# A two-stage kernel (gated linear attention, then an MLP): attention in chunks of 64 tokens of two batch rows, its products in quarter and half tiles of the array, TensorE in written order

## Chip, core, metric

One core of a Trainium2 chip runs the whole program. Its engines work side by side and wait for each other by semaphores: TensorE (PE, matrix products into PSUM; a product is a load of a stationary operand of up to 128 rows and 128 columns, PEld in the profile, and a pass of moving columns over it), VectorE (DVE), ScalarE (ACT), GpSimd (POOL) and SyncE (SP, which here only issues DMAs). The metric is device time in microseconds, lower is better.

## What is computed

For 4 batch rows and 8 heads an mLSTM cell with a 40x40 state runs over 768 tokens; its output, gated, goes through a two-layer MLP with SiLU. Cut to what matters:

```python
for t in range(S):
    m_new = np.maximum(f_gate[:, :, t] + m, i_gate[:, :, t])
    f_stab = np.exp(f_gate[:, :, t] + m - m_new)
    i_stab = np.exp(i_gate[:, :, t] - m_new)
    m = m_new
    C = f_stab[..., None, None] * C + i_stab[..., None, None] * np.einsum('bhd,bhe->bhde', vt, kt)
    n = f_stab[..., None] * n + i_stab[..., None] * kt
    h = np.einsum('bhde,bhe->bhd', C, qt)
    denom = np.maximum(np.abs(np.einsum('bhd,bhd->bh', n, qt)), 1.0)[..., None]
    y[:, :, t] = h / (1.0 + np.exp(-o_gate[:, :, t])) / denom
x = y.transpose(0, 2, 1, 3).reshape(3072, 320)
h = x @ w_in                                   # 320 x 2048
out = (h / (1.0 + np.exp(-h))) @ w_out         # 2048 x 320
```

All data are f32; the answer is f32.

## The kernel before

The recurrence is done by chunks. A *unit* is 128 tokens of one batch row with all 8 heads; there are 24 (6 chunks by 4 batch rows; unit n is chunk n // 4 of batch row n % 4). Per unit and head, *scores* multiply k by q (L392; 128 tokens of k by 128 of q), VectorE multiplies them with the tile D of decays (L411), and *values* multiply the weighed D with v that carries a column of ones (41 columns, L431). From the second chunk on the product of decayed q with the carried state Cm is added in the same PSUM tile (L422). *State* multiplies k with the decayed v (L461; three heads to a product, of which only the diagonal blocks are wanted, so VectorE masks them with bm, L487), and Cm is decayed and summed up on GpSimd (L472, L488). D starts as a broadcast DMA of the log decays (L277); GpSimd masks it (L353) and ScalarE takes eight exponentials with a bias each (L363). The 8 first units (LIGHT) keep q and k in f32 in 40 of 64 rows, half the heads in each half of the rows; all later units split q and k into a rounded part and a remainder (ScalarE L336, VectorE L338), stacked to 120 rows, so that one product of the fp32r kind does.

VectorE turns a unit's values into x: nq, den, the division, the output gate and a copy (L437 to L453). Three *transposes* (L494) and a split into two fp32r parts (L496, L497) hand x to the MLP.

The MLP works in 8 *steps* of 3 units (384 tokens). A step has 16 chunks fc of 128 hidden columns. The first products of a chunk are 8 (L526, 384 moving columns, called mm1), the second ones, two chunks later, 9 (L566, 320 moving columns, called mm2; in step 0 three in plain f32). Between them ScalarE and VectorE make th, gh and gl (L530 to L546; in step 0 only th and g).

Weights come as float64 bits and are unpacked by VectorE and ScalarE in 18 parts (L182 to L217; wti and wto are its tiles); the calls are written in front of the loop over steps and within the first chunks of step 0.

What sets the order: SyncE's DMAs go in written order. The other engines are put in order by the framework's scheduler, which works with priorities and its own estimates of duration. The units are cut in 5 pieces (`piece`, L611), and a table SCHED says how many pieces are due by which chunk of which step. Tiles come from rotating pools; psA, which holds scores, values, state and transposes, has three PSUM banks.

## Time and profile before

| | us |
|---|---|
| device time, median of 3 runs (526.55 to 527.87) | 527.78 |
| span of the profiled execution, first to last instruction | 521.3 |
| TensorE busy (matmul / weight load) | 482.5 / 462.5 |
| VectorE, ScalarE, GpSimd busy | 343.1, 267.8, 98.6 |
| first MLP product | 60.4 |
| first second product of step 1 | 134.3 |
| last matmul ends | 516.96 |

The page gives no time for the profiled execution but its span; what the runs show above it (6.5 us to the median) lies before the first and after the last instruction. The ends of matmuls are modelled and overlap the next one's start, so the cost of a group is read from the start of its first to the start of the next group. An f32 product stands in the trace as two pairs of load and matmul, an fp32r product as one.

### The profile page before, as it was taken

To read this page: it belongs to the slowest core of one execution; us is meant where nothing else is said; L and a number is where in the kernel's file an instruction comes from. 1 tells how busy PE (TensorE), PEld (TensorE's weight loads), DVE (VectorE), ACT (ScalarE), POOL (GpSimd) and SP (SyncE) were. 2 spreads that over 40 slices of the span, in tenths; PEclk is the share of its full clock that TensorE was granted. 3 is DMA by queue.
4 is the path that set the end of the run, shared out by engine and by line. 5 is a ranking of instruction groups with operands and counts; after the bars stand their busy time and mean duration, and the time that the engine had idled before them with its cause. 6 is when DMAs were issued, how large, how long until landed. Compare 5 with 4: busy or idle time off the path is not lost.

```text
span 521.3 us, 8616 instructions
## 1 busy us (share of the span) xinstructions
PE 482.5 (93%) x3086; PEld 462.5 (89%) x3086; DVE 343.1 (66%) x717; ACT 267.8 (51%) x647; POOL 98.6 (19%) x139
## 2 busy tenths in 40 slices
PE   1477899999999979998999999999999999999996
PEld 1376878788989969998999999999999999999996
DVE  6579999945777678586865866449575745454332
ACT  1554776532765556575465564446464433334332
POOL 0121232231333422332203211121210000000000
PEclk9999999999999999999999999999999999999999
DMA  4999975163476385746513543433570100001001
GB/s 108 319 322 265 273 268 157 40 183 93 124 188 183 108 201 150 214 127 155 157 67 106 156 105 107 115 108 104 152 209 18 28 14 26 0 2 39 0 2 38
DMA packets 52525, 65.54 MB, mean 126 GB/s; under 512 B 3195, under 2 KB 40479, under 8 KB 52483
## 3 DMA queue, kind: packets, MB, share of 16 engines
q1 hardware_dynamic: 48963, 60.95, 41.6%
q10 hardware_dynamic: 3520, 4.04, 2.2%
q8 instruction: 24, 0.39, 0.3%
q14 instruction: 18, 0.15, 0.1%
HBM read 60.94 MB, written 4.04 MB: 125 GB/s over the span
## 4 chain that ended last, share of the span: by engine, by line
PE 59%; DMA 19%; DVE 11%; ACT 5%; issue 2%; SPq 1%; POOL 1%; POOLq 0%; ACTq 0%; DVEq 0%
PE ph L526 25%; PE pout L566 24%; DMA D<-LFd 12%; PE po L431 5%; DMA raw<-in_qk_dram 4%; DVE st L338 3%; ACT D L363 3%; PE ps L392 2%; DMA kvo<-in_kvo_dram 2%; PE po L422 2%; POOL D L353 1%; DVE D L411 1%; ACT st L336 1%; PE px L494 1%; PE pu L461 1%
## 5 line engine op out<-in xcount | busy, mean ns | idle before, releaser
L526 PE MATMUL ph<-xh,wh 128*128 128x384 f32 x384 | 136.1, 354 | 3.3 <-DVE th L539 2.3
L526 PE MATMUL ph<-xl,wh 128*128 128x384 f32 x384 | 130.6, 340 | 0.0
L566 PE MATMUL pout<-woh,gh 128*128 128x320 f32 x336 | 106.6, 319 | 3.0 <-ACT gh L544 3.0
L539 DVE SCALAR_TENSOR_TENSOR th<-th,ph 128x384 f32<-128x384 f32 x112 | 61.5, 549 | 70.1 <-ACT th L530 69.8
L566 PE MATMUL pout<-wol,gh 128*128 128x320 f32 x336 | 103.2, 309 | 0.0
L566 PE MATMUL pout<-woh,gl 128*128 128x320 f32 x336 | 100.4, 313 | 1.3 <-DVE gl L545 1.2
L545 DVE TENSOR_TENSOR gl<-th,gh 128x384 fp32r<-128x384 f32 x112 | 65.0, 582 | 54.3 <-ACT gh L544 52.4
L530 ACT ACTIVATE th<-ph 128x384 f32<-128x384 f32 x128 | 62.0, 485 | 62.2 <-PE ph L526 61.0
L526 PE MATMUL ph<-xh,wl 128*128 128x384 f32 x256 | 87.4, 342 | 0.0
L544 ACT CAST gh<-th 128x384 fp32r<-128x384 f32 x112 | 57.1, 510 | 51.2 <-DVE th L539 49.6
L526 PEld LDWEIGHTS ph<-xh,wh 128*128 128x128 f32 x384 | 73.0, 190 | 6.7 <-DVE th L539 3.4
L526 PEld LDWEIGHTS ph<-xl,wh 128*128 128x128 f32 x384 | 73.0, 190 | 0.6
L363 ACT ACTIVATE D<-D,aT 128x128 f32<-128x128 f32 x192 | 59.8, 390 | 17.1 <-POOL D L353 17.0
L566 PEld LDWEIGHTS pout<-woh,gh 128*128 128x128 f32 x336 | 63.2, 188 | 4.9 <-ACT gh L544 4.8
L566 PEld LDWEIGHTS pout<-woh,gl 128*128 128x128 f32 x336 | 61.7, 188 | 2.6 <-DVE gl L545 2.3
L566 PEld LDWEIGHTS pout<-wol,gh 128*128 128x128 f32 x336 | 63.2, 188 | 0.1
L431 PEld LDWEIGHTS po<-kvo,D 128*128 128x128 f32 x384 | 53.3, 215 | 3.3 <-ACT wh L203 2.1
L431 PE MATMUL po<-kvo,D 128*128 128x41 f32 x384 | 54.3, 299 | 1.9 <-ACT wh L203 1.9
L353 POOL TENSOR_SCALAR_AFFINE_SELECT D<-D 128x512 f32<-128x512 f32 x48 | 36.8, 790 | 91.6 <-ACT fd L350 66.2
L338 DVE TENSOR_TENSOR st<-raw,st 40x512 fp32r<-40x512 f32 x64 | 45.9, 717 | 7.1 <-ACT st L336 5.6
L526 PEld LDWEIGHTS ph<-xh,wl 128*128 128x128 f32 x256 | 48.7, 190 | 0.0
L336 ACT CAST st<-raw 120x512 fp32r<-120x512 f32 x64 | 35.7, 621 | 17.0 <-DMA raw<-in_qk_dram 17.0
(74 smaller groups left out, 548.2 us busy)
## 6 DMA issues: line engine op xcount, KB each, us to landing
raw<-in_qk_dram SPq DMA_DIRECT2D x32, 480.0 KB
D<-LFd SPq DMA_DIRECT2D x24, 512.0 KB
kvo<-in_kvo_dram SPq DMA_DIRECT2D x24, 484.0 KB
wro<-in_w_out_dram SPq DMA_DIRECT2D x8, 640.0 KB
wri<-in_w_in_dram SPq DMA_DIRECT2D x8, 512.0 KB
out_dram<-ob ACTq DMA_DIRECT2D x24, 160.0 KB
qt<-in_qp_dram SPq DMA_DIRECT2D x20, 180.0 KB
lq<-LFd SPq DMA_DIRECT2D x60, 60.0 KB
```

Source lines behind the costliest of these rows:

```text
L336: nc.scalar.copy(t, raw)
L338: nc.vector.tensor_tensor(out=t[r0 : r0 + D, :], in0=raw[r0 : r0 + D, :], in1=t[r0 : r0 + D, :].bitcast(F32), op=ALU.subtract,)
L353: nc.gpsimd.affine_select(out=d, in_=d, compare_op=ALU.is_ge, fill=NEG, base=0, pattern=[[0, HH], [1, L]], channel_multiplier=-1,)
L363: nc.scalar.activation(d[:, h, :], d[:, h, :], AF.Exp, bias=aT[:, c, r + h : r + h + 1])
L392: nc.tensor.matmul(ps[:, j, :], k_[:, cs], q_[:, cs], start=True, stop=True)
L431: nc.tensor.matmul(po[:, h, :], self.Dm[:, h, :], self.vt[:, h, :], start=first, stop=(h == H - 1))
L526: nc.tensor.matmul(ph, w, x, start=(i == 0), stop=(i == len(ops) - 1))
L530: nc.scalar.activation(th, ph, AF.Tanh, scale=0.5)
L539: nc.vector.scalar_tensor_tensor(out=th, in0=th, scalar=1.0, in1=ph, op0=ALU.add, op1=ALU.mult)
L544: nc.scalar.copy(gh, th)
L545: nc.vector.tensor_tensor(out=gl, in0=th, in1=gh.bitcast(F32), op=ALU.subtract)
L566: nc.tensor.matmul(self.po[t], g[:, ts], w, start=(fc == 0 and i == 0), stop=(last and i == len(ops) - 1),)
```

## The change

A unit is now 64 tokens of two batch rows (a pair p), again 128 rows, with 8 heads of each; there are again 24 (12 chunks by 2 pairs; unit n is chunk n // 2 of pair n % 2), so the carried state passes from unit n to unit n + 2 in place of n + 4. The 16 (batch row, head) combinations are laid out in 8 slots; everything stays f32 and the split of q and k is gone.

- *Scores* (L376 of the changed kernel): 16 products of 64x64 tokens; heads lie in two halves of the rows and batch rows in two halves of the columns. D is 128x8x64, half as large.
- *Values* (L408): 8 products whose stationary operand has 64 columns, written to one half of the PSUM rows; the moving operand v holds the two batch rows block-wise, the other block zero, 2x41 columns. The carried state is a product of the same form (qt against Cm, 104 rows).
- *State* (L443): 8 products with 40 stationary columns; here k, not v, is decayed (kw). No mask is needed. Decaying Cm stays on GpSimd (L456), the addition moves to VectorE (L462).
- *Decay*: `shift` adds mask and gates on GpSimd ahead of time, `decay` adds the loaded log decays, one exponential does all 8 heads.
- q comes once; the decayed q is made from the same tile, so the load of qp is gone. k with o, and v, are loaded apart; outputs are stored by two DMAs.
- *Order*: from the loop over steps on TensorE runs in the order in which the program is written. `piece` k = 0 of unit n now issues the scores of unit n + 1 and then values and state of unit n; k = 1 the transposes; `shift` and `decay` are for unit n + 2. The scores of unit 3 move ahead of the loop.

On TensorE, one unit within a later step; pu, po, ps, px, ph and pout are state, values, scores, transposes, mm1 and mm2. Before (values of one unit, a group of mm1 and its state; its transposes and the scores of the next unit stand elsewhere):

```order
L422 MATMUL po_2269<-Cm_106,qt_1773 128x123 x2
L422 MATMUL po_2269<-Cm_106,qt_1773 128x82
L431 MATMUL po_2269<-kvo_1771,D_1765 128x41 x8
L566 MATMUL pout_2_2151<-wol_1229,gh_3_2173 128x320
L566 MATMUL pout_2_2151<-woh,gl_3_2174 128x320
L526 MATMUL ph_6_2305<-xh_1190,wh 128x384
...
L526 MATMUL ph_6_2305<-xl_1191,wh 128x384
L461 MATMUL pu_2321<-vw_2196,kvo_1771 120x123 x2
L461 MATMUL pu_2321<-vw_2196,kvo_1771 80x82
L566 MATMUL pout_0_2149<-woh,gh_4_2231 128x320
```

And now (of the 16 rows of scores the first two):

```order
L500 MATMUL ph_2_2870<-xl_1770,wh 128x384
L376 MATMUL ps_0_2898<-qk_2639 64x64
L376 MATMUL ps_1_2899<-qk_2639 64x64
...
L408 MATMUL po_2920<-Cm_113,qt_2770 64x2x41 x8
L408 MATMUL po_2920<-vb_114,D_2423 64x2x41 x8
L443 MATMUL pu_2947<-vb_114,kw_2666 40x2x41 x8
L540 MATMUL pout_0_2960<-woh,gh_0_2818 128x320
...
L500 MATMUL ph_3_2972<-xl_1770,wh 128x384
L468 MATMUL px_2992<-ident,x_2943 128x128 x3
L540 MATMUL pout_0_2960<-woh,gh_1_2845 128x320
```

The parts of a unit that stood apart are now one block, and the transposes stand one group of mm2 and one of mm1 behind it.

On VectorE, at the end of the unpacking of weights in step 0 (wo is the last result of a part; x of unit 4 is x_809 before and x_848 now; g_5 to g_8 and g_6 are results of mm1 in step 0). Before:

```order
L534 SCALAR_TENSOR_TENSOR g_7_827<-th_7_825,ph_7_816 128x384
L487 TENSOR_TENSOR ut_2_838<-pu_829,bm 80x82
L447 TENSOR_TENSOR x_809<-po_791,den_803 128x320
L184 TENSOR_SCALAR wto_759<-wto_759 128x640
L450 SCALAR_TENSOR_TENSOR x_809<-kvo_446,x_809 128x320
L204 TENSOR_TENSOR wl<-wti_751,wh 128x2x256
L187 SCALAR_TENSOR_TENSOR wto_759<-wro_657,wto_759 128x640
L534 SCALAR_TENSOR_TENSOR g_8_862<-th_8_860,ph_8_851 128x384
L453 COPY x_809<-x_809 128x64
L193 SCALAR_TENSOR_TENSOR wo_764<-wro_657,wto_759 128x640
```

And now:

```order
L422 RECIPROCAL den_842<-den_842 128x8
L225 TENSOR_TENSOR wl<-wti_888,wh 128x2x256
L208 SCALAR_TENSOR_TENSOR wto_896<-wro_758,wto_896 128x640
L427 TENSOR_TENSOR x_848<-po_825,den_842 128x320
L214 SCALAR_TENSOR_TENSOR wo_901<-wro_758,wto_896 128x640
L245 TENSOR_TENSOR wol_1327<-wo_493,woh 128x640
L430 SCALAR_TENSOR_TENSOR x_848<-ko_498,x_848 128x320
L433 COPY x_848<-x_848 128x64
L471 TENSOR_TENSOR xl_642<-px_905,xh_641 128x3x128
L245 TENSOR_TENSOR wol_1469<-wo_561,woh 128x640
L508 SCALAR_TENSOR_TENSOR g_6_925<-th_6_923,ph_6_914 128x384
```

The last unpacking (wo_764, now wo_901) came behind g_8; now it comes ahead of g_6, and x of unit 4 is finished right behind it.

On TensorE, what stands behind that x, in step 0 (ph_5 and ph_6 are mm1, px the transposes of unit 4):

```order
L500 MATMUL ph_5_868<-xh_311,wh 128x384
...
L500 MATMUL ph_5_868<-xl_312,wh 128x384
L468 MATMUL px_905<-ident,x_848 128x128 x3
L540 MATMUL pout_0_700<-wo_493,g_3_717 128x320
L540 MATMUL pout_1_701<-wo_493,g_3_717 128x320
L540 MATMUL pout_2_702<-wo_493,g_3_717 128x320
L500 MATMUL ph_6_914<-xh_311,wh 128x384
```

In the written order mm1 number 6 follows the transposes of unit 4; before, these stood behind mm1 number 9.

The diff, cut:

```diff
 B, H, S, D = 4, 8, 768, 40
-L = 128
+L = 64
 NC = S // L
-NU = NC * B
+NP = B // 2
+NU = NC * NP
 DM = H * D
 DFF = 2048
 NFC = DFF // 128
 UPS = 3
-NT = UPS * L
+UT = 2 * L
+NT = UPS * UT
 NSTEP = NU // UPS
 D1 = D + 1
-GRP = [(0, 3), (3, 3), (6, 2)]
-KS = 3 * D
+HD1 = H * D1
+KS = 64 + D
...
-LIGHT = range(8)
...
+        two = pb.tile([BH, c1 - c0, 2, L], F32, tag="two", bufs=1, name=f"two{lo}")
+        for k in range(2):
+            eng.tensor_tensor(
+                out=two[:, :, k, :],
+                in0=i_t[:, lo:hi].rearrange("r (c t) -> r c t", t=L),
+                in1=LF[:, lo:hi].rearrange("r (c t) -> r c t", t=L),
+                op=ALU.subtract,
+            )
...
-    Cm = [cp.tile([KS, 3, 3 * D1], F32, name=f"Cm{b}") for b in range(B)]
-    HH = H // 2
+    Cm = [cp.tile([KS, 2, HD1], F32, name=f"Cm{p}") for p in range(NP)]
+    vb = [cp.tile([128, 2, HD1], F32, name=f"vb{k}") for k in range(3)]
+    for t in vb:
+        for k in range(2):
+            nc.gpsimd.memset(t[k * L : (k + 1) * L, 1 - k, :], 0.0)
+    for t in Cm:
+        nc.gpsimd.memset(t, 0.0)
...
             self.Dm = p3.tile([128, H, L], F32, tag="D", name=f"D{n}")
-            nc.sync.dma_start(
-                self.Dm, LFd[b, 0:H, sl].unsqueeze(0).broadcast_to([128, H, L])
-            )
+            for k in range(2):
+                r = p * 2 * H + k * H
+                nc.sync.dma_start(
+                    self.Dm[k * L : (k + 1) * L],
+                    LFd[c, r : r + H, :].unsqueeze(0).broadcast_to([L, H, L]),
+                )
...
+            t = pb.tile([KS, 2, H * L], F32, tag="big", name=f"qk{n}")
+            nc.sync.dma_start(t.rearrange("p w t -> p (w t)"), qk[n])
+            self.q = t[:, 0, :].rearrange("p (h t) -> p h t", t=L)
+            self.k = t[:, 1, :].rearrange("p (h t) -> p h t", t=L)
...
+            t = p3.tile([128, 2 * DM], F32, tag="ko", name=f"ko{n}")
+            nc.sync.dma_start(t, ko[n])
+            self.kt = t[:, :DM].rearrange("p (h e) -> p h e", e=D)
+            self.ot = t[:, DM:].rearrange("p (h e) -> p h e", e=D)
+            v = vb[n % 3]
+            for k in range(2):
+                r = slice(k * L, (k + 1) * L)
+                nc.sync.dma_start(v[r, k, :], vp[n, r, :])
+            self.vt = v.rearrange("p k (h e) -> p k h e", e=D1)
...
+                self.lq = p2.tile([KS, H, L], F32, tag="lq", name=f"lq{n}")
+                lf = LFd[c, p * 2 * H : (p + 1) * 2 * H, :].rearrange(
+                    "(d a e) t -> a d (e t)", d=2, a=2
+                )
+                to = self.lq.rearrange("p (d e) t -> p d (e t)", d=2)
+                for k, r in ((0, slice(0, 64)), (1, slice(64, KS))):
+                    w = r.stop - r.start
+                    nc.sync.dma_start(to[r], lf[k].unsqueeze(0).broadcast_to([w, 2, 4 * L]))
...
-        def split(self, hf, which):
...
+        def shift(self):
+
+            self.am = p2.tile([128, H, L], F32, tag="am", name=f"am{self.n}")
+            nc.gpsimd.tensor_tensor(
+                out=self.am,
+                in0=mask.unsqueeze(1).broadcast_to([128, H, L]),
+                in1=aT[:, self.c, self.p, :].unsqueeze(2).broadcast_to([128, H, L]),
+                op=ALU.add,
+            )
+
+        def decay(self):
+            nc.gpsimd.tensor_tensor(out=self.Dm, in0=self.Dm, in1=self.am, op=ALU.add)
+            nc.scalar.activation(self.Dm, self.Dm, AF.Exp)
...
-                nc.gpsimd.tensor_tensor(out=self.qt, in0=self.qt, in1=self.lq, op=ALU.mult)
+                self.qt = p2.tile([KS, H, L], F32, tag="qt", name=f"qt{self.n}")
+                nc.gpsimd.tensor_tensor(out=self.qt, in0=self.q, in1=self.lq, op=ALU.mult)
...
+            ps = [
+                psA.tile([128, H // 2, L], F32, tag="a", name=f"ps{n}_{a}") for a in range(2)
+            ]
+            for j in range(4):
+                for d in range(2):
+                    for a in range(2):
+                        r = slice(a * 64, a * 64 + D)
+                        nc.tensor.matmul(
+                            ps[a][d * L : (d + 1) * L, j, :],
+                            self.k[r, d * 4 + j, :],
+                            self.q[r, d * 4 + j, :],
+                            start=True,
+                            stop=True,
+                        )
+            if self.c < NC - 1:
...
+                self.kw = p2.tile([128, H, D], F32, tag="kw", name=f"kw{n}")
...
+                    in0=self.kt,
+                    in1=self.Dm[:, :, L - 1].unsqueeze(2).broadcast_to([128, H, D]),
                     op=ALU.mult,
                 )
-            hs = slice(hf * HH, (hf + 1) * HH)
-            nc.vector.tensor_tensor(
-                out=self.Dm[:, hs, :], in0=ps, in1=self.Dm[:, hs, :], op=ALU.mult
-            )
+            for a in range(2):
+                d = self.Dm[:, a * 4 : (a + 1) * 4, :]
+                nc.vector.tensor_tensor(out=d, in0=ps[a], in1=d, op=ALU.mult)
...
+            by_d = po.rearrange("p (a d e) f -> p a e d f", a=2, d=2)
+            by_a = po.rearrange("p (a d e) f -> p d e a f", a=2, d=2)
+            ops = []
             if c > 0:
-                for g, (h0, nh) in enumerate(GRP):
+                cm = Cm[p].rearrange("p a (h e) -> p a h e", e=D1)
+                ops += [(by_a, self.qt, cm, d, e) for d in range(2) for e in range(2)]
+            ops += [(by_d, self.Dm, self.vt, a, e) for a in range(2) for e in range(2)]
+            for i, (to, w, m, x, e) in enumerate(ops):
+                for g in range(2):
+                    j = x * 4 + e * 2 + g
                     nc.tensor.matmul(
-                        flat[:, h0 * D1 : (h0 + nh) * D1],
...
+                        to[g * L : (g + 1) * L, x, e],
+                        w[:, j, :],
+                        m[:, :, j, :],
+                        start=(i == 0),
+                        stop=(i == len(ops) - 1),
...
+            pu = bank(n, psO, "o", [128, H, D1], f"pu{n}")
+            by_d = pu.rearrange("p (d j) f -> p j d f", d=2)
+            for j in range(4):
+                for a in range(2):
+                    nc.tensor.matmul(
+                        by_d[a * 64 : a * 64 + D, j],
+                        self.kw[:, a * 4 + j, :],
+                        self.vt[:, :, a * 4 + j, :],
+                        start=True,
+                        stop=True,
                     )
...
-                    tmp = cp.tile([KS, 2, 3 * D1], F32, tag="utmp", name=f"ut{n}_{g0}")
-                    tv = tmp[:K, : g1 - g0, : nh * D1]
-                    nc.vector.tensor_tensor(out=tv, in0=u, in1=msk, op=ALU.mult)
-                    nc.gpsimd.tensor_tensor(out=v, in0=v, in1=tv, op=ALU.add)
+                    nc.vector.tensor_copy(v, pu[r])
+                    continue
+                nc.gpsimd.tensor_tensor(
+                    out=v,
+                    in0=v,
+                    in1=self.lq[r, :, L - 1].unsqueeze(2).broadcast_to([D, H, D1]),
+                    op=ALU.mult,
+                )
+                nc.vector.tensor_tensor(out=v, in0=v, in1=pu[r], op=ALU.add)
...
+            for k in range(2):
+                r = (2 * p + k) * S + c * L
+                nc.scalar.dma_start(out[r : r + L, :], ob[k * L : (k + 1) * L])
...
@@ -615,22 +570,33 @@
         if k == 0:
             if n + 2 < NU:
                 units[n + 2].load()
-            u.scores()
-        elif k == 2:
+            if n + 1 < NU:
+                units[n + 1].scores()
             u.values()
-        elif k == 3:
             u.state()
-        elif k == 4:
+        elif k == 1:
+            if n + 2 < NU:
+                units[n + 2].shift()
             if n % UPS == 0:
                 steps[n // UPS] = Step(n // UPS)
             u.xpose(steps[n // UPS])
-        prep(n + 1, k)
-
+        elif k == 2:
+            if n + 1 < NU:
+                units[n + 1].misc()
+        elif k == 3:
+            if n + 2 < NU:
+                units[n + 2].decay()
...
+    units[3].scores()
+    units[4].shift()
+    units[4].decay()
+
+
+    ctx.enter_context(tc.manual_schedule(engines={mybir.EngineType.PE}))
...
```

More of the change, by code (lines that the diff above doesn't have):

```diff
@@ L117, in gates @@
             nc.vector.memset(f_t[:, 0:1], 0.0)
-        for c in range(lo // L, hi // L):
+        for c in range(c0, c1):
             sl = slice(c * L, (c + 1) * L)
@@ L380, in scores @@
-            for j in range(HH):
-                for hf in range(2):
-                    self.score(ps[hf], hf, j)
-            for hf in range(2):
-                self.weigh(ps[hf], hf)
-        def bank_s(self, hf):
-            return psA.tile([128, HH, L], F32, tag="a", name=f"ps{self.n}_{hf}")
-        def score(self, ps, hf, j):
-            q_, k_ = self.st[hf]
-            cs = slice(j * L, (j + 1) * L)
-            nc.tensor.matmul(ps[:, j, :], k_[:, cs], q_[:, cs], start=True, stop=True)
@@ L394, in half @@
-        def half(self, hf):
-            ps = self.bank_s(hf)
-            for j in range(HH):
-                self.score(ps, hf, j)
-            self.weigh(ps, hf)
-        def weigh(self, ps, hf):
-            n = self.n
-            if hf == 0 and self.c < NC - 1:
-                self.vw = p2.tile([128, H, D1], F32, tag="vw", name=f"vw{n}")
+            n = self.n
+            ps = [
+                psA.tile([128, H // 2, L], F32, tag="a", name=f"ps{n}_{a}") for a in range(2)
+            ]
```

249 lines of the change are left out of this document (70 added, 179 removed).

## The prediction

> **What bounds the kernel now.** I read the page first, then the timeline of the matmuls, then busy time by stage, then the waits. The page:
>
> ```profile
> span 521.3 us, 8616 instructions
> PE 482.5 (93%) x3086; PEld 462.5 (89%) x3086; DVE 343.1 (66%) x717; ACT 267.8 (51%) x647; POOL 98.6 (19%) x139
> ```
>
> Busy time by stage says where TensorE is the limit and where VectorE is:
>
> ```profile
> core 0: us, PE busy (x) PEld busy (x) DVE busy (x) ACT busy (x) POOL busy (x), PEclk, DMA share, GB/s
> 40.00:60.00 20.00, 14.96 (x70) 13.18 (x69) 19.79 (x49) 11.39 (x30) 3.67 (x4) 1.00 0.99 281
> 60.00:84.00 24.00, 22.94 (x123) 20.12 (x123) 23.88 (x47) 16.52 (x36) 6.77 (x7) 1.00 0.67 212
> 84.00:100.00 16.00, 15.38 (x81) 12.16 (x80) 15.83 (x33) 10.13 (x28) 6.14 (x7) 1.00 0.48 139
> 134.00:521.00 387.00, 376.44 (x2519) 370.66 (x2519) 239.62 (x492) 199.48 (x479) 67.11 (x96) 1.00 0.37 100
> ```
>
> From 40 to 100 us VectorE is full (59.5 of 60 us; it unpacks the weights); from 134 us on TensorE is, with VectorE at 62% and the DMA engines at 37%. What a stage of TensorE costs is read from starts, because durations of matmuls overlap. In the tail:
>
> ```profile
> 470.81 0.34 PE L526 MATMUL ph<-xh,wh 128*128 128x384 f32 x1
> ...
> 472.23 0.31 PE L566 MATMUL pout<-woh,gh 128*128 128x320 f32 x1
> ...
> 473.54 0.34 PE L526 MATMUL ph<-xh,wh 128*128 128x384 f32 x1
> ```
>
> One chunk of the hidden layer is 1.42 us of first products and 1.31 us of second ones, 2.73 us together. At 134 us, counted from the listing, 109 groups of the first and 112 of the second kind are left: 112 x 2.73 - 3 x 1.42 = 301.5 us. After the last product
>
> ```profile
> 513.29 3.67 PE pout L566 x25
> ```
>
> (from the chain; it ends at 516.96) come 4.3 us of output. So 387 - 301.5 - 4.3 = 81 us go to the 17 units whose values are still to come, 4.8 us each. The parts of one unit, in the same listing (each part lasts until the next row starts):
>
> ```profile
> 123.25 0.79 PE L422 MATMUL po<-Cm,qt 120*128 120x123 f32 x6
> 123.87 1.92 PE L431 MATMUL po<-kvo,D 128*128 128x41 f32 x16
> 125.62 1.86 PE L566 MATMUL pout<-wo,g 128*128 128x320 f32 x6
> ...
> 128.71 0.73 PE L461 MATMUL pu<-vw,kvo 128*120 128x123 f32 x6
> 129.27 1.82 PE L566 MATMUL pout<-wo,g 128*128 128x320 f32 x6
> ...
> 210.59 0.49 PE L494 MATMUL px<-ident,x 128*128 128x128 f32 x3
> 210.83 1.09 PE L392 MATMUL ps<-st 120*128 120x128 f32 x8
> 211.75 0.36 PE L566 MATMUL pout<-woh,gl 128*128 128x320 f32 x1
> ```
>
> Carried-state product 0.62, values 1.75, state 0.56, transposes 0.24, scores 0.92: 4.09 us. The other 0.7 us per unit is waits and changes of kind.
>
> **The change on TensorE.** The listing counts pairs of weight load and matmul; an f32 product is two pairs (8 products in L431 are x16). The changed unit has 16 score products (32 pairs), 8 carried-state, 8 value and 8 state products (16 pairs each): 80 pairs in place of 36. What a smaller pair costs is bounded by these rows:
>
> ```profile
> 69.93 1.78 PE L566 MATMUL pout<-wo,g 128*128 128x320 f32 x6
> 71.54 0.27 PE L494 MATMUL px<-ident,x 128*128 128x128 f32 x1
> ...
> 116.03 1.16 PE L392 MATMUL ps<-raw 40*128 40x128 f32 x16
> 117.12 1.88 PE L566 MATMUL pout<-wo,g 128*128 128x320 f32 x6
> ...
> 134.56 1.16 PE L392 MATMUL ps<-raw 40*128 40x128 f32 x8
> 135.65 0.42 PE L566 MATMUL pout<-wol,gh 128*128 128x320 f32 x1
> ```
>
> Six f32 pairs with 320 moving columns take 1.61 us: 0.84 ns a column, so 82 columns are 69 ns and 64 are 54. Sixteen value pairs in 1.75 us, 109 ns, stream only 41 columns (34 ns): there the load of 128 weight columns is the limit, 0.85 ns a column, so 64 columns load in 54 ns. The last two blocks are the key. When the scores of the early units alternate between the two halves of the rows, a pair takes 1.09/16 = 68 ns; when four products in a row sit in one half (eight pairs), 1.09/8 = 136 ns. Two row tiles overlap completely.
>
> Scores after: 64x64 tiles, alternating row halves for each product and column halves for every second. One tile alone would be 136/2 = 68 ns; two row tiles make it 34, all four tiles 17. 32 x 34 = 1.09 us, lower bound 0.54, upper 2.2. I take 1.09: only rows are shown to overlap.
>
> Carried state, values, state after: 128x64 tiles that alternate between column halves, 82 moving columns. No row shows column tiles. Upper bound 69 ns (streams one after another), lower 34 (two at once). I take 38, nearer the lower end, because the two row tiles overlapped fully: 48 x 38 = 1.82 us, bounds 1.63 and 3.31.
>
> With the transposes (0.24) the unit is 3.15 us in place of 4.09. The 0.7 us of waits and changes of kind I keep, since a block enters and leaves tile shapes three times while the present kernel cuts a unit into four or five blocks. The saving is 0.94 x 17 = 16 us.
>
> **The written order.** The transposes of a unit now come one chunk after its state: the cover is state (0.6 us) plus 2.73 us. They need VectorE's x, whose steps are nq, three den with two additions of the state between them, the next kw, two for x and a copy:
>
> ```profile
> L437 DVE TENSOR_SCALAR nq<-po 128x8 f32<-128x8 f32 x24 | 3.8, 158 | 4.9 <-PE po L431 4.9
> L438 DVE SCALAR_TENSOR_TENSOR den<-nq 128x8 f32<-128x8 f32 x24 | 3.9, 164 | 0.5
> L441 DVE TENSOR_SCALAR den<-den 128x8 f32<-128x8 f32 x24 | 6.6, 274 | 0.5
> L404 DVE TENSOR_TENSOR vw<-kvo,D 128x328 f32<-128x328 f32 x20 | 11.2, 559 | 9.2 <-ACT D L363 9.2
> L442 DVE RECIPROCAL den<-den 128x8 f32<-128x8 f32 x24 | 4.8, 198 | 0.4
> L447 DVE TENSOR_TENSOR x<-po,den 128x320 f32<-128x320 f32 x24 | 11.7, 487 | 0.4
> L450 DVE SCALAR_TENSOR_TENSOR x<-kvo,x 128x320 f32<-128x320 f32 x24 | 13.9, 581 | 0.4
> L453 DVE COPY x<-x 128x64 f32<-128x64 f32 x24 | 7.2, 300 | 0.5
> L472 POOL TENSOR_TENSOR Cm<-Cm,fd 120x246 f32<-120x246 f32 x16 | 11.6, 726 | 103.4 <-PE po L422 103.4
> L371 POOL TENSOR_TENSOR qt<-qt,lq 120x384 f32<-120x384 f32 x20 | 21.5, 1075 | 89.2 <-ACT lq L370 82.5 <-DVE vw L404 6.7
> L411 DVE TENSOR_TENSOR D<-ps,D 128x512 f32<-128x512 f32 x48 | 32.0, 682 | 1.4 <-PE ps L392 1.1
> ```
>
> With an estimated 0.45 for each addition (328 elements against the 320 of L447) that is about 3.6 us against 3.3 us of cover: 0.3 us of wait per unit, 17 x 0.3 = 5 us. The additions also wait for two POOL products of 40x328, by L472 726 x 328/246 = 0.97 us each, which start after the carried-state products and so end about 0.5 us after the state's matmuls; that is inside the sum only if POOL has nothing else.
>
> **Step 0.** Every weight part is unpacked by VectorE. Two rows, of TensorE's and of VectorE's listing:
>
> ```profile
> 83.46 0.42 PE L526 MATMUL ph<-xh,wh 128*128 128x384 f32 x1
> ...
> 97.19 0.81 DVE L193 SCALAR_TENSOR_TENSOR wo<-wro,wto 128x640 uint32<-128x640 uint32 x1
> ```
>
> The last unpacking ends at 98.0 us. In the new VectorE order x of unit 4 stands one product and two rows of x behind that same last unpacking, and the written TensorE order puts its transposes ahead of first products 6. Before, the seventh group (number 6) started at 83.46 us with the scores of unit 5 still to do. VectorE saves until there ten weighings of half length (L411, 10 x 0.34 = 3.4 us), three products g of th and ph that now come later (1.5 us) and some 2 us of late decay tiles, because each D is half as large and takes one exponential in place of eight. So about 98 - 6 = 92 us, 8 us later than 83.5; less the 3 us of products that are then already done, and less the slack that the present kernel still had there, I book 5 us lost, bounds 0 and 10.
>
> **What goes under cover.** ScalarE loses the splits and seven of eight exponentials per unit, VectorE the subtractions and half the weighing: from 134 us on neither is the limit, so I count nothing. POOL gets two additions and one product of 512 columns, 1.4 us each by 1075 ns for 384 (L371 above), some 6 us a unit against 20 us between units. Loads shrink, 0.37 of DMA time already free. The doubled output DMAs lie on ScalarE's queue with 4.3 us after the last product, unchanged within 0.2.
>
> **Sum.** -16 + 5 (waits for x) + 5 (step 0), and 2 x 0.94 = 1.9 less for units 5 and 6, which also run after VectorE is free: -7.9 us, a span of 513.4. The runs' median 527.78 lies 6.5 above the profiled span, so 520 us. With the pairs of a unit at their lower bounds (2.17 us for 2.91) it is 506; with 3.3 us, column tiles saving a third of 69 ns, it is 527.
>
> **Rivals.**
> 1. *Column tiles do not overlap.* For: no row shows them, and both halves read all 128 rows. Against: row tiles overlapped fully. 3.31 + 1.09 + 0.24 = 4.64 us, 0.55 more than 4.09, over 19 units +10, and 10 for waits and step 0: 548 us. It decides from 46 ns a pair, where 0.55 us saved a unit just pay those 10.
> 2. *Pairs never go below the 68 ns seen.* For: no pair in the trace is shorter. [...]
>
> ```profile
> 31.65 2.08 PE L392 MATMUL ps<-raw 40*128 40x128 f32 x16
> 33.66 1.93 PE L431 MATMUL po<-kvo,D 128*128 128x41 f32 x8
> ```
>
> 80 x 68 ns = 5.44 us, with the transposes 1.6 more than 4.09: +30 + 10, 568 us.
> 3. *The order eats the gain.* POOL's two products, late behind one of its 1.4 us operations, hold VectorE's additions, these hold x, and TensorE waits at the transposes. For: the three stand in one chain in the written order. Against: by the count above POOL works 6 us of every 20. From 0.47 us a unit over the 0.3 booked the gain is gone; 0.55 gives 529.
> 4. *All four score tiles run together and step 0 loses nothing:* 0.54 for 1.09 us, -10, and -5: 505.
> 5. *In column tiles a load waits for the stream before it.* 54 + 69 = 123 ns, 48 pairs 5.9 us, 3.1 more than 4.09 with scores and transposes: +60 + 10, 598. Against: in the whole array they overlap (the value pairs, 109 ns where 109 and 34 would add to 143). [...]
>
> **How the numbers follow.** Forecast 0.45, rival 1 0.20, 2 0.07, 3 0.16, 4 0.10, 5 0.02. A run of this kernel tells 0.3% (1.6 us) from no change. Faster: 0.45 + 0.10 + 0.02 of rival 3 = 0.57; same: 0.08 of rival 3; slower: 0.20 + 0.07 + 0.02 + 0.06 of rival 3 = 0.35. The likeliest case's own range is 506 to 527; to leave out no more than 2 in 10 it goes from 500 to 548, which takes in rivals 1, 3 and 4.
>
> **What would show it.** Right: blocks of 16 value pairs in about 0.6 us, 32 score pairs in about 1.1, a unit near 4 us from 134 us on. Wrong: 1.1 us for a block of value pairs (rival 1), 2.2 for scores (rival 2), many waits of TensorE at the transposes for x behind POOL's Cm (rival 3). Step 0: first products 6 should start near 92 us; near 84 would make 515 of it.

## The result, and the profile after

The changed kernel takes 542.89 us (median of 4 runs, 542.06 to 544.2) against 527.83 (526.55 to 533.89) for the kernel before: a ratio of 1.0295, 95% interval 1.0252 to 1.0337. It is 3% slower; 520 us had been forecast. The profiled execution is one of 542.31 us with a span of 540.4, so 19.1 us of span have to be found (before: 521.3). Two of the profiled executions below are longer than the medians that stand beside them: that of run 1 (667 us, at a granted clock of 0.67), of which no stage is read, and that of run 2 (570.2 us against 563.2).

The page, with the fortieths of the span (13.5 us a digit) for TensorE and its granted clock:

```profile
span 540.4 us, 10327 instructions
PE 446.9 (83%) x4068; PEld 417.7 (77%) x4068; DVE 331.6 (61%) x669; ACT 196.6 (36%) x397; POOL 133.2 (25%) x129
PE   1532419269998998899999999899999999999995
PEclk9966658779999999999999999899999999999999
```

TensorE has 982 instructions more and 35.6 us less of busy time; its share falls from 93% to 83%. The work did become cheaper. The loss stands in the first ten digits, the first 135 us, where TensorE was 75 to 100% busy from 40 us on before. Two of the prediction's stages and the next one, in the busy time by stretch (the columns are those of the prediction's table):

```profile
40.00:60.00 20.00, 4.66 (x71) 3.22 (x67) 19.81 (x37) 7.72 (x15) 7.62 (x5) 0.59 1.01 254
60.00:84.00 24.00, 10.82 (x102) 9.49 (x103) 20.29 (x34) 8.87 (x17) 8.58 (x6) 0.57 0.49 158
100.00:134.00 34.00, 20.92 (x159) 17.13 (x160) 22.06 (x41) 8.32 (x16) 5.91 (x6) 0.80 0.16 40
```

From 40 to 60 us VectorE is as full as before (19.81 us) but gets through 37 instructions in place of 49, GpSimd is busy 7.62 us in place of 3.67, and TensorE 4.66 in place of 14.96. The granted clock of 0.59 is not what sets the two kernels apart there. The prediction's table has 1.00 for the kernel before, but its rows show half the pace there too: sixteen score pairs of one shape took 2.01 us at 31.65 us and 1.09 at 116.03, and that kernel's first products follow each other at 0.32 us up to 66 us and at 0.175 after (the changed kernel's at 0.32 from 61.70 to 63.30 us). Why the early products take about twice as long is not shown.

The cut between step 0 and the rest is best laid at the last group of first products of step 0 (number 15 of 0 to 15), which stands at the same place of the written order in every kernel with that order. The kernel before isn't in that order: ahead of its group 15 lie values and state of 6 units, in the changed kernel of 7, and one unit's scores more as well. So up to 2.5 us of each of the two differences below are work that moved across the cut. In TensorE's listing of the changed kernel, with a unit's blocks far behind step 0:

```profile
112.39 0.88 PE L468 MATMUL px<-ident,x 128*128 128x128 f32 x3 [13.94 <-DVE x L430]
...
115.73 0.58 PE L500 MATMUL ph<-xh,wh 128*128 128x384 f32 x1
...
149.44 0.58 PE L500 MATMUL ph<-xh,wh 128*128 128x384 f32 x1
...
302.61 0.69 PE L376 MATMUL ps<-qk 40*64 40x64 f32 x32
303.23 0.79 PE L408 MATMUL po<-Cm,qt 104*64 104x82 f32 x16
303.85 0.74 PE L408 MATMUL po<-vb,D 128*64 128x82 f32 x16
304.42 0.73 PE L443 MATMUL pu<-vb,kw 128*40 128x82 f32 x16
...
310.63 0.49 PE L468 MATMUL px<-ident,x 128*128 128x128 f32 x3
```

and the row of the kernel before that answers to the third:

```profile
118.60 0.58 PE L526 MATMUL ph<-xh,wh 128*128 128x384 f32 x1
```

Group 15 starts at 149.4 us in place of 118.6: **step 0 loses 30.8 us**. From there to the end it is 391.0 us in place of 402.7: **the rest gains 11.7**. The unit itself is now 0.62 + 0.62 + 0.57 + 0.67 (to the row behind it, 305.09) + 0.25 = 2.73 us in place of 4.09. Group 6 starts at 115.7 us where the prediction wanted 92, behind 13.9 us of waiting for x. The stretch ahead of step 0 (the head) loses nothing: group 0 starts at 59.9 us, before at 60.4.

What made x late there is seen in VectorE's listing from x's first step (nq) on:

```profile
97.94 0.15 DVE L417 TENSOR_SCALAR nq<-po 128x8 f32<-128x8 f32 x1
98.01 1.00 DVE L462 TENSOR_TENSOR Cm<-Cm,pu 40x328 f32<-40x328 f32 x2
...
100.73 2.45 DVE L418 SCALAR_TENSOR_TENSOR den<-nq 128x8 f32<-128x8 f32 x1
103.10 0.48 DVE L385 TENSOR_TENSOR kw<-ko,D 128x320 f32<-128x320 f32 x1
103.51 1.52 DVE L208 SCALAR_TENSOR_TENSOR wti<-wri,wti 128x512 uint32<-128x512 uint32 x1
...
109.89 0.48 DVE L427 TENSOR_TENSOR x<-po,den 128x320 f32<-128x320 f32 x1
110.29 0.82 DVE L214 SCALAR_TENSOR_TENSOR wo<-wro,wto 128x640 uint32<-128x640 uint32 x1
...
111.76 0.49 DVE L430 SCALAR_TENSOR_TENSOR x<-ko,x 128x320 f32<-128x320 f32 x1
112.28 0.20 DVE L433 COPY x<-x 128x64 f32<-128x64 f32 x1
```

and GpSimd's listing of the same stretch:

```profile
100.55 1.39 POOL L365 TENSOR_TENSOR qt<-qk,lq 104x512 f32<-104x512 f32 x1 [2.88 <-ACT lq L363]
101.90 1.26 POOL L357 TENSOR_TENSOR D<-D,am 128x512 f32<-128x512 f32 x1
103.23 1.25 POOL L349 TENSOR_TENSOR am<-mask,aT 128x512 f32<-128x512 f32 x1
```

Two things stand there. The steps of x lie far apart, with unpackings between them: 14 us from nq to the copy. And the second step, on 8 columns, takes 2.45 us where such an operation took 0.164 (the prediction's row L438): it starts at 100.73, while GpSimd's product of 100.55 runs, and ends at 103.18, when GpSimd's next operation ends. L208 behind it does the same with the third: 1.52 us, where 0.68 is its usual time, and its end (105.03) comes 0.55 behind GpSimd's (104.48).

The list of waits of the changed kernel names what TensorE waits for; behind step 0 (149.4 us to the end) three are left:

```profile
PE px L468 <- DVE x L430: 8.6, 13, 0.8
PE pout L540 <- ACT ob L557: 5.3, 5, 2.2
PE pu L443 <- DVE D L393: 2.0, 3, 0.9
```

(engine, line, what it waits for: us in all, times, the longest.) Over the whole span the first is 48.4 us. Of the other 39.8 us, 18.6 lie in the head, where TensorE's order is still the scheduler's, and 21.2 in step 0: 6.5 at the transposes of unit 3, 13.9 at those of unit 4, 0.7 at those of unit 5. Another 7.0 us of step 0 are waits of the state products for VectorE's weighing of D.

### The profile page after: what moved, and what is told of

It is laid out like the page before. It is cut to its first block, busy times and chain, and to the rows that moved or that the text cites. A ratio compares the mean times of both kernels' runs of the same rounds, so it can differ in the third digit from the quotient of the medians.

```text
span 540.4 us, 10327 instructions
## 1 busy us (share of the span) xinstructions
PE 446.9 (83%) x4068; PEld 417.7 (77%) x4068; DVE 331.6 (61%) x669; ACT 196.6 (36%) x397; POOL 133.2 (25%) x129
## 3 DMA queue, kind: packets, MB, share of 16 engines
q1 hardware_dynamic: 24228, 43.79, 29.7%
## 4 chain that ended last, share of the span: by engine, by line
issue 29%; PE 23%; DMA 19%; DVE 13%; POOL 9%; SPq 4%; ACT 3%; ACTq 1%; POOLq 0%; DVEq 0%
PE ph L500 11%; PE pout L540 10%; DMA ko<-in_ko_dram 5%; DMA lq<-LFd 5%; POOL Cm L456 4%; DMA D<-LFd 4%; POOL D L357 3%; POOL am L349 2%; DMA qk<-in_qk_dram 2%; SPq L338 2%; DMA wri<-in_w_in_dram 1%; DVE wo L214 1%; SPq L304 1%; DVE D L393 1%; DVE Cm L462 1%
## 5 line engine op out<-in xcount | busy, mean ns | idle before, releaser
L500 PE MATMUL ph<-xl,wh 128*128 128x384 f32 x384 | 132.1, 344 | 0.6 <-DVE xl L471 0.6
L519 DVE TENSOR_TENSOR gl<-th,gh 128x384 fp32r<-128x384 f32 x112 | 77.2, 690 | 63.2 <-ACT gh L518 61.4
L540 PE MATMUL pout<-woh,gl 128*128 128x320 f32 x336 | 104.0, 310 | 0.0
L456 POOL TENSOR_TENSOR Cm<-Cm,lq 40x328 f32<-40x328 f32 x40 | 33.9, 847 | 176.1 <-PE po L408 158.0
L540 PEld LDWEIGHTS pout<-woh,gl 128*128 128x128 f32 x336 | 63.3, 188 | 0.3 <-DVE gl L519 0.3
L468 PE MATMUL px<-ident,x 128*128 128x128 f32 x72 | 14.5, 307 | 50.7 <-DVE x L430 48.4
L468 PEld LDWEIGHTS px<-ident,x 128*128 128x128 f32 x72 | 8.6, 151 | 56.7 <-issue 33.4
L365 POOL TENSOR_TENSOR qt<-qk,lq 104x512 f32<-104x512 f32 x22 | 30.2, 1371 | 89.9 <-ACT lq L363 70.7
L363 ACT ACTIVATE lq<-lq 104x512 f32<-104x512 f32 x22 | 13.9, 630 | 79.6 <-DMA lq<-LFd 79.6
L357 POOL TENSOR_TENSOR D<-D,am 128x512 f32<-128x512 f32 x24 | 34.6, 1444 | 10.7 <-DMA D<-LFd 10.0
```

The source lines that it names most:

```text
L357: nc.gpsimd.tensor_tensor(out=self.Dm, in0=self.Dm, in1=self.am, op=ALU.add)
L363: nc.scalar.activation(self.lq, self.lq, AF.Exp)
L365: nc.gpsimd.tensor_tensor(out=self.qt, in0=self.q, in1=self.lq, op=ALU.mult)
L456: nc.gpsimd.tensor_tensor(out=v, in0=v, in1=self.lq[r, :, L - 1].unsqueeze(2).broadcast_to([D, H, D1]), op=ALU.mult,)
L468: nc.tensor.transpose(px[:, c, :], self.x[:, c, :], ident)
L500: nc.tensor.matmul(ph, w, x, start=(i == 0), stop=(i == len(ops) - 1))
```

## The experiments

Two theories came out of these listings. **A, the order:** TensorE, in written order, waits at the transposes for an x that VectorE's queue delivers late. **B, the additions:** VectorE itself is slower, because its instructions take longer beside GpSimd's additions of 512 columns; then TensorE's order only shows it. All times below are medians; the kernel before, run beside them, had 527.8, 528.6 and 528.9.

**1. TensorE's order left to the scheduler**

```diff
-    ctx.enter_context(tc.manual_schedule(engines={mybir.EngineType.PE}))
```

> The tiles with TensorE's order left to the scheduler, as the kernel before has it; nothing else is changed. Theory A (the written TensorE order makes TensorE wait in step 0 and at every unit's transposes for values that VectorE delivers late): most of the 32 us of step 0 and of the 16 us of waits at the transposes go; first products 6 start below 92 us, the time is 505 to 520 us. Rival B (VectorE itself needs longer, because its instructions take longer beside GpSimd's new additions of 512 columns; TensorE's order only shows it): first products 6 still start after 100 us, the time is 528 to 542 us.

Measured: 521.11 us, ratio to the kernel before 0.985 (0.979 to 0.990). The order is a cause: without it the tiles are faster than the kernel before, by 1.5%. Its stages are read in run 10, the same kernel once more.

**2. The written order alone, on the old tiles**

```diff
+    ctx.enter_context(tc.manual_schedule(engines={mybir.EngineType.PE}))
     done = 5 * UPS
```

> The kernel before, with its old tiles, with TensorE in written order from step 0 on: the order alone. Theory A: first products 6 start after 100 us in place of 83.5 and the time rises to 545 us or more. Rival B: GpSimd is as light as before, so VectorE keeps its pace and the written order costs little: 528 to 535 us.

Measured: 563.24 us, ratio 1.064 (1.058 to 1.070). A written order costs the old tiles more than the new. Not as A had it, though: group 6 started at 87.3 us and group 15 at 128.8, 10 us late, and the larger part, 37.0 us in this execution of 570.2, is lost behind step 0, where TensorE's waits are up to 4 us long; the most, 13.1 us, are for ScalarE's output copies (ob). One wait for gl, in TensorE's listing:

```profile
321.93 0.42 PE L566 MATMUL pout<-woh,gl 128*128 128x320 f32 x1 [2.18 <-DVE gl L545]
...
323.05 0.51 PE L526 MATMUL ph<-xh,wh 128*128 128x384 f32 x1
323.36 0.52 PE L526 MATMUL ph<-xl,wh 128*128 128x384 f32 x1
...
326.56 0.31 PE L566 MATMUL pout<-woh,gh 128*128 128x320 f32 x1
```

Behind a wait of 2.18 us the first products follow each other at 0.32 us in place of 0.175, for some 3.4 us; the granted clock is 0.51 from 323.1 to 326.5 us and 1.00 ahead of the wait. So this wait was followed by some 3.4 us at little more than half the rate; what lowers the clock is not shown.

**3. No additions on GpSimd** (the causal mask and the column term of the decay are left out, so that part isn't computed)

```diff
-            self.am = p2.tile([128, H, L], F32, tag="am", name=f"am{self.n}")
-            nc.gpsimd.tensor_tensor(
-                out=self.am,
...
-            )
+            return
...
-            nc.gpsimd.tensor_tensor(out=self.Dm, in0=self.Dm, in1=self.am, op=ALU.add)
             nc.scalar.activation(self.Dm, self.Dm, AF.Exp)
```

> The changed kernel without GpSimd's two additions of 512 columns per unit (the causal mask and the column term of the decay are left out, so the computation is not the reference's in this part). Theory A: TensorE's order stays and its waits with it, 535 to 543 us. Rival B: the unpacking rows of VectorE (128x640) come back from 1189 ns to about 810, the 12 us that they and their like gained go, first products 6 start near 100 us and the time is 520 to 530 us.

Measured: 532.42 us, 10.5 less than the changed kernel (ratio to the kernel before 1.007, 1.004 to 1.010). The unpacking row among the groups of VectorE's instructions up to 116 us (the last numbers are us in all, ns of one, idle time before), first of the changed kernel and then of this one:

```profile
L214 DVE SCALAR_TENSOR_TENSOR wo<-wro,wto 128x640 uint32<-128x640 uint32 x8 | 9.5, 1189 | 0.0
```

```profile
L214 DVE SCALAR_TENSOR_TENSOR wo<-wro,wto 128x640 uint32<-128x640 uint32 x8 | 6.5, 817 | 0.0
```

The end of the unpacking in VectorE's listing of this run, and the start of group 15 in TensorE's:

```profile
101.45 0.82 DVE L214 SCALAR_TENSOR_TENSOR wo<-wro,wto 128x640 uint32<-128x640 uint32 x1
```

```profile
140.07 0.58 PE L493 MATMUL ph<-xh,wh 128*128 128x384 f32 x1
```

1189 ns become 817, the kernel before's 814. The last unpacking ends at 102.3 us in place of 111.1 and group 15 starts at 140.1 in place of 149.4. The additions are a cause too, of 9.4 us up to group 15; 5.9 of them come in the head (group 0 starts at 54.0 us in place of 59.9). The time is 2 us above B's 530, and the waits for x stay large (35.8 us on the page).

The row's mean hides how it comes about. Of the eight unpackings in the changed kernel five take 809 to 819 ns, and three, each beside a GpSimd instruction with two operands, 1658 to 1904 (one of the three beside the product qt alone, which is no addition). Summed up from the durations of the trace up to 116 us: the 26 instructions of VectorE that ran mainly beside one of the two additions took some 14 us more than the shortest of their line and shape, the 123 that ran beside no GpSimd instruction 1.3 us more in all. That leaving out the additions also lets GpSimd finish D sooner was not tried apart.

**4. Transposes three pieces later**

```diff
         elif k == 1:
...
-            if n % UPS == 0:
-                steps[n // UPS] = Step(n // UPS)
-            u.xpose(steps[n // UPS])
+        elif k == 4:
+            if n % UPS == 0:
+                steps[n // UPS] = Step(n // UPS)
+            u.xpose(steps[n // UPS])
```

> The changed kernel with a unit's three transposes written three pieces later (as its fifth piece, where the kernel before has them), so that three chunks of the hidden layer lie between the state's products and the transposes. Theory A: the waits of TensorE at the transposes for x (48 us in all) go nearly to nothing, of which 16 us lie after 116 us and the rest in step 0: 505 to 515 us. Rival B: in step 0 VectorE still ends its unpacking at 111 us, so only the 16 us of the later steps go: 525 to 530 us.

Measured: 520.77 us, ratio 0.985 (0.980 to 0.989): between the theories, and faster than the kernel before, with the written order kept. Its waits, and the start of group 15 in TensorE's listing:

```profile
PE px L468 <- DVE x L430: 13.8, 3, 9.0
PE ph L500 <- DVE g L508: 8.4, 3, 4.2
```

```profile
132.64 0.58 PE L500 MATMUL ph<-xh,wh 128*128 128x384 f32 x1
```

Step 0 gets 16.8 us back. Nearly all that is left of the waits for x (4.4 and 9.0 us) lies before the first group of first products (58.3 us); a new one, for g, has come in, since g stands in the same queue of VectorE. Behind group 15 the gain is only 3.4 us (387.6); there TensorE has two stretches of 6.8 us at a granted clock of 0.50 (from 194.7 and 321.0 us), the changed kernel one of 3.4.

**5. The same tiles without alternation**

```diff
-            for j in range(4):
+            for a in range(2):
                 for d in range(2):
-                    for a in range(2):
+                    for j in range(4):
...
-            for i, (to, w, m, x, e) in enumerate(ops):
-                for g in range(2):
+            for g in range(2):
+                for i, (to, w, m, x, e) in enumerate(ops):
```

(and the state's products by row half `a` first).

> The changed kernel with the same 80 pairs a unit and the same tiles, but neighbouring products no longer alternate between row halves or column halves of the array (scores: four products in one 64x64 tile, then the next tile; values and state: all products of one column half, then of the other). Theory A (what made the pairs short, 19 ns for scores and 36 to 39 for values, is that neighbours in different tiles run at once): 32 score pairs take about 2.2 us in place of 0.62 (68 ns each), 16 value pairs about 1.1 in place of 0.6; some 3 us more a unit, 17 units behind step 0, 580 to 600 us. Rival B (small tiles are short in themselves, whatever stands beside them): the blocks keep 0.6 us and the time stays at 540 to 546 us.

Measured: 564.14 us, 21 above the changed kernel. A unit behind step 0:

```profile
312.42 1.54 PE L376 MATMUL ps<-qk 40*64 40x64 f32 x32
313.89 0.78 PE L408 MATMUL po<-Cm,qt 104*64 104x82 f32 x8
...
315.96 0.84 PE L443 MATMUL pu<-vb,kw 128*40 128x82 f32 x13
316.72 0.42 PE L540 MATMUL pout<-woh,gh 128*128 128x320 f32 x1
```

32 score pairs take 1.47 us (46 ns each) in place of 0.62 (19 ns); the 48 other pairs 2.83 (59 ns) in place of 1.86 (39 ns). So neighbours in different tiles do overlap, both in the 48 pairs that alternate in the columns alone and in the 32 that alternate in rows and columns: A in its kind, but a lone tile is shorter than the 68 and 69 ns that it was given. A unit is 1.8 us longer; behind group 15 the loss is 20.5 us (411.5), and the wait for x there falls from 8.6 us to 0.3, which fits a longer unit that gives VectorE more time.

**6. Late transposes, and the decay as the kernel before makes it**

```diff
-            nc.gpsimd.tensor_tensor(out=self.Dm, in0=self.Dm, in1=self.am, op=ALU.add)
-            nc.scalar.activation(self.Dm, self.Dm, AF.Exp)
+            for k in range(2):
+                d = self.Dm[k * L : (k + 1) * L]
+                nc.gpsimd.affine_select(
+                    out=d, in_=d, compare_op=ALU.is_ge, fill=NEG, base=0,
+                    pattern=[[0, H], [1, L]], channel_multiplier=-1,
+                )
+            for h in range(H):
+                nc.scalar.activation(
+                    self.Dm[:, h, :], self.Dm[:, h, :], AF.Exp,
+                    bias=aT[:, self.c, self.p, h : h + 1],
+                )
```

> The kernel with late transposes, and with the decay made as the kernel before makes it: GpSimd selects the causal half (one operand, two instructions of 64 partitions) and ScalarE takes eight exponentials with the column term as bias; the two additions of 512 columns are gone. Theory A (GpSimd's two-operand additions stretch VectorE's unpacking, and that is a cost of its own beside TensorE's order): the 128x640 unpacking row returns to about 815 ns, the last unpacking ends near 96 us in place of 104.5, and the time is 509 to 514 us. Rival B (with the transposes late, VectorE's extra time is hidden under TensorE): 518 to 522 us. Rival C (ScalarE's seven more exponentials a unit come late): above 524 us.

Measured: 521.19 us, ratio 0.985 (0.980 to 0.990): no gain over run 4. The last unpacking did end 3.8 us earlier (100.6 for 104.5), less than A's 8. The selections take 863 ns each and hold VectorE up too: of the eight unpackings of 128x640 (mean 868 ns, not 815) one ran beside two selections and took 1.27 us, the seven others 0.77 to 0.83. In VectorE's and in GpSimd's listing:

```profile
52.97 1.27 DVE L214 SCALAR_TENSOR_TENSOR wo<-wro,wto 128x640 uint32<-128x640 uint32 x1
```

```profile
51.87 1.70 POOL L353 TENSOR_SCALAR_AFFINE_SELECT D<-D 64x512 f32<-64x512 f32 x2
```

But TensorE's wait for g, in the list of waits, rose from 8.4 us to 12.7; the longest of these waits in TensorE's listing stands below it:

```profile
PE ph L503 <- DVE g L511: 12.7, 2, 8.0
```

```profile
76.21 0.69 PE L503 MATMUL ph<-xh,wh 128*128 128x384 f32 x1 [8.00 <-DVE g L511]
```

This is group 3. First products have two PSUM buffers, so in the written order group 3 needs the one that g of group 1 frees, and group 7 that of group 5. TensorE comes to the wait earlier than in run 4 (the second products ahead of it start at 66.4 us for 72.7), and g of group 1 ends 2.5 us earlier (76.2 for 78.6); but g of group 5 does not (99.8 for 99.3), so group 7 starts at 99.9 us for 99.3, and the gain is gone. Why g of group 5 comes no sooner, when VectorE has less to do, was not tried apart; VectorE's own order is the scheduler's, planned anew for each kernel.

**7. The old decay, TensorE's order left to the scheduler**

> The same decay as in the run before, and TensorE's order left to the scheduler (transposes in their place of the changed kernel). Theory A (both causes are independent): 521.1 less the 8 to 10 us of the additions, 510 to 514 us. Rival B (the scheduler already hides VectorE's extra time): 519 to 522 us.

Its edit is that of run 6 for the decay and that of run 1 for the order. Measured: 510.09 us, ratio 0.965 (0.959 to 0.971): A. Group 15 in TensorE's listing and the last unpacking in VectorE's:

```profile
123.13 0.45 PE L503 MATMUL ph<-xh,wh 128*128 128x384 f32 x1
```

```profile
111.37 0.82 DVE L214 SCALAR_TENSOR_TENSOR wo<-wro,wto 128x640 uint32<-128x640 uint32 x1
```

From group 15 it is 384.2 us to the end. The same lighter GpSimd that gave nothing in the written order gives 11 us where TensorE's order is the scheduler's. The last unpacking ends at 112.2 us, later than in the changed kernel (111.1), and group 15 starts 26.3 us sooner: a late end of the unpacking is not the loss in itself, only what stands behind it in a fixed order.

**8. Late transposes, and no additions** (mask and column term left out as in run 3)

> Late transposes and no additions on GpSimd at all (mask and column term of the decay left out, so that part isn't computed): a bound on what the additions can cost when TensorE's order waits less. If the two causes add up: 520.8 - 10.5 = 510 us and first products 6 near 84 us, as before the change. If the waits at the transposes were only the sign of a late VectorE: 518 to 521 us.

Measured: 513.24 us, ratio 0.972 (0.965 to 0.980). The last unpacking in VectorE's listing and group 15 in TensorE's:

```profile
94.80 0.82 DVE L214 SCALAR_TENSOR_TENSOR wo<-wro,wto 128x640 uint32<-128x640 uint32 x1
```

```profile
123.46 0.58 PE L493 MATMUL ph<-xh,wh 128*128 128x384 f32 x1
```

Group 15 starts at 123.5 us, 26.0 before the changed kernel's. Run 4 alone gave 16.8 and run 3 alone 9.4, together 26.2: at group 15 **the two causes add up**. In the times they do so less closely, 22.1 and 10.5 us alone and 29.7 together (the profiled execution took 509.0 us). Group 6 starts at 88.2, not near 84, and at group 15 4.9 us against the kernel before are left.

**9. The kernel before, with two additions on GpSimd**

```diff
             r = b * H + hf * HH
+            nc.gpsimd.tensor_tensor(
+                out=d, in0=d, in1=zero.unsqueeze(2).broadcast_to([128, HH, L]), op=ALU.add
+            )
```

> The kernel before, with two GpSimd additions of 512 columns per unit more (each half of the decay tile plus zero, in place, ahead of its selection; the result is the same). Theory A (such additions stretch VectorE's instructions, whatever else the kernel does): the 128x640 unpacking row goes from 814 ns to 1000 or more, the last unpacking ends 6 to 10 us later than 98.0, and the time rises by 8 to 12 us, 536 to 540. Rival B (what stretched VectorE in the changed kernel was something else in it, its tile shapes or its DMAs): the row stays at 814 to 830 ns and the time within 3 us of the kernel before.

Measured: 546.73 us, ratio 1.037 (1.030 to 1.045). The unpacking rows up to 125 us of this kernel, and then of the kernel before:

```profile
L193 DVE SCALAR_TENSOR_TENSOR wti<-wri,wti 128x512 uint32<-128x512 uint32 x8 | 10.1, 1267 | 0.0
L193 DVE SCALAR_TENSOR_TENSOR wo<-wro,wto 128x640 uint32<-128x640 uint32 x8 | 8.1, 1018 | 0.0
```

```profile
L193 DVE SCALAR_TENSOR_TENSOR wo<-wro,wto 128x640 uint32<-128x640 uint32 x8 | 6.5, 814 | 0.0
L193 DVE SCALAR_TENSOR_TENSOR wti<-wri,wti 128x512 uint32<-128x512 uint32 x8 | 5.9, 737 | 0.0
```

A, and more than A had: the last unpacking ends at 111.1 us in place of 98.0. In the profiled execution (540.2 us) group 15 starts 5.9 us later, and another 11.2 us go behind it, where VectorE isn't full. There TensorE waits 11.7 us in place of 6.8, and its granted clock is 0.50 from 171.2 to 174.6 and from 212.1 to 218.9 us; how the additions bring these about was not tried. Two additions a unit that change no result make the old kernel as slow as the changed one.

**10. Run 1 again, for its profile**

> The same kernel as in the first run (the tiles, TensorE's order left to the scheduler), for a profile that was not disturbed: time 519 to 523 us. Theory A (the order is one cause, GpSimd's additions the other): first products 6 start near 95 us, first products 15 near 133, and the stretch from there to the end is near the 387 us that late transposes gave, 16 less than the 402.7 of the kernel before. Rival B (the order costs only the waits behind step 0): first products 15 near 149 as in the changed kernel, and 372 us from there.

Measured: 522.38 us. Group 6 starts at 93.1 us and group 15 at 130.6 (A: 95 and 133):

```profile
130.56 0.44 PE L500 MATMUL ph<-xh,wh 128*128 128x384 f32 x1
```

From there it is 390.1 us, 12.6 us less than the kernel before, not 16.

**11. Scheduler, old decay and late transposes**

> TensorE's order by the scheduler, the old decay, and the transposes three pieces later. Theory A (the scheduler already fills the wait at the transposes): no change from 510.1, within 2 us. Rival B (where the transposes stand in the program still counts, because the scheduler's priorities follow it): 504 to 508 us.

Measured: 509.94 us, ratio 0.966 (0.960 to 0.971): A. With the scheduler's order, the place of the transposes in the program is worth nothing here.

**12. Scheduler, old decay and a third buffer for lq**

```diff
-                self.lq = p2.tile([KS, H, L], F32, tag="lq", name=f"lq{n}")
+                self.lq = p3.tile([KS, H, L], F32, tag="lq", name=f"lq{n}")
```

> TensorE's order by the scheduler, the old decay, and a third buffer for lq, so that its load does not stand in SyncE's queue until GpSimd's product of two units before, with the weight loads behind it. Theory A (SyncE's queue is not the limit, VectorE is): no change from 510.1, within 2 us. Rival B (the blocked queue holds weights back in step 0): the 9 us of waits of that queue in step 0 come back in part, 504 to 508 us.

Measured: 518.23 us, ratio 0.981 (0.976 to 0.987): 8 us slower than without it, which neither theory had. Group 15 starts 2 us later (125.2) and the rest is 7.6 us longer. In TensorE's listing from 125 us on the score products stand in 51 separate pieces in place of 35 and take 18.0 us in place of 14.4, so the scheduler planned another order. Why a buffer makes it do that stays open.

## Why the prediction was wrong, step by step

**Tiles: right, and too careful.** Scores were booked at 34 ns a pair, because only row tiles had been seen to overlap; four tiles in turn took 19 ns, against 46 without alternation (run 5), which is the first half of rival 4, whose bound was 17. Pairs in column halves were booked at 38 ns and took 39. The unit came to 2.73 us for 3.15. Run 5 shows that alternation makes it so. Rivals 1, 2 and 5 fall with it. For rival 5 it is the 39 ns of column halves in turn against 59 of one half after another: tiles of the same rows overlap as well. The 68 ns of rival 2 were no floor: the score pairs took 19.

**Behind step 0: near in sum, by luck.** Booked were -16 for the tiles, -1.9 for two more units and +5 for x, -12.9; measured, -11.7. But a unit saves 1.36 us where 0.94 was booked, which makes -23 over 17 units, and the written order takes back more than was booked: the waits for x came to 8.6 us in place of 5, and 7.3 us had no term, 5.3 for the output copies of ScalarE (ob), which the next step's second products wait for, and 2.0 for D. These terms give -7; the unit that moved across the cut is 2.5 of what is missing, and the rest stays open. Where the scheduler removed nearly all waits (run 7), the same stretch gained 18.5.

**Step 0: the failed term.** Booked were 5 us with bounds 0 and 10; it was 30.8. Two steps of the prediction failed.

- "So about 98 - 6 = 92 us", for the last unpacking and with it group 6, took VectorE's durations from the kernel before. The unpacking ended at 111.1, group 6 started at 115.7. GpSimd's additions had been priced by GpSimd's own load ("some 6 us a unit against 20 us between units") and counted as covered. What they cost is not GpSimd's time but VectorE's, in the one stretch where VectorE has none to spare: 9.4 us (run 3). The duration rows of a trace held for the neighbours that they were taken with: the 128x640 unpacking took 814 ns in the kernel before, 1189 here and 817 without the additions; den took 2.45 us for 0.164, ending with GpSimd's operation (103.18 and 103.16 us). What makes VectorE slower beside GpSimd is not shown.
- Only the transposes of unit 4, ahead of group 6, were priced, at what the late unpacking costs x. In step 0 the written order held TensorE for x at the transposes of units 3, 4 and 5, 21.2 us in all, 13.9 of them at unit 4, where x's steps lay 14 us apart in VectorE's queue. Moving the transposes alone gave 16.8 us back (run 4).

With both causes out (run 8), group 15 starts 4.9 us later than before. That this is about the 5 us that were booked is chance: there the transposes no longer stand ahead of group 6, which starts at 88.2 us, before the last unpacking ends (95.6). What is left has another make-up. Group 0 starts at 53.1 us, 7.3 sooner than before, and from there to group 15 it takes 70.4 us in place of 58.2, with 10.3 us of TensorE's waits (for D, x, g and xl) in place of 1.7. What makes VectorE late in that stretch with both causes out was not tried.

**Rival 3 had the place, not the mechanism.** It saw waits at the transposes and gave 529 us, but blamed GpSimd's two products on the carried state for holding VectorE's additions. These two additions took 1.00 us together in the listing above, near the 0.45 each that the prediction had for their work, and the list of VectorE's waits has none for GpSimd; what held x was VectorE's own queue of unpackings, and GpSimd's operations as VectorE's neighbours (den, 2.45 us for 0.164).

**The sum with the measured terms:** +30.8 (order 16.8, additions 9.4, the rest 4.6) - 11.7 = 19.1 us of span.

## What to carry to other kernels

Price an instruction that is moved to GpSimd by what VectorE does at that time: 18 additions of some 1.4 us up to 116 us, 25.4 us of GpSimd's time, cost 9.4 us up to group 15 through a full VectorE, and two additions a unit of no use made the kernel before 3.7% slower, a third of it up to group 15. Before an engine's order is written by hand, look at each wait that it fixes in the stage where the engine that it waits for is full; the same tiles were 3% slower than the kernel before in one written order, 1.5% faster with three instructions a unit moved three pieces on, and 3.5% faster (510 us) with the order left to the scheduler and GpSimd relieved. A cheaper stage is worth its price only if what feeds it can follow: the unit lost a third of its time on TensorE, and step 0 gave back more than that.

## What was not expected of the hardware

- An operation of 8 columns on VectorE took 2.45 us for 0.164, beside two GpSimd instructions in a row. Two selections with one operand on GpSimd held VectorE up as well (run 6: an unpacking of 1.27 us where the others took 0.77 to 0.83).
- Four 64x64 tiles in turn give 19 ns a pair where one tile takes 46; two column halves of 128x64 give 39 ns where one takes 59.
- TensorE's granted clock was 0.57 to 0.59 from 40 to 84 us of the changed kernel, where it was 23 to 45% busy, and products ran at 0.32 us in place of 0.175 for some 3.4 us behind a wait of 2.18 us (run 2; in the 3.4 us ahead of the slow stretch TensorE was busy 36% of the time).
